# Spectral mixer plus MLP on one core: kept splits of the spectral weights and matrices, and 47-point groups spread over the steps of the unit ahead

## The chip, the cores and the metric

The kernel runs on one core of one Trainium2 chip. The metric is the time of the program on the device in microseconds (us), lower is better. A core has TensorE (PE in the profile, its weight loads as PEld), VectorE (DVE), ScalarE (ACT), GpSimd (POOL) and SyncE (SP), which here only issues transfers. ACT issues transfers too.

## The reference

Inputs are x of 8 x 3008 x 256 and weights in float32. What is computed, cut to what matters:

```python
X = np.fft.rfft(x, axis=1)                      # over the 3008 positions
Yr = Xr @ w_r - Xi @ w_i + b_r
Yi = Xr @ w_i + Xi @ w_r + b_i
Yr, Yi = soft_threshold(Yr, 0.01), soft_threshold(Yi, 0.01)
x = np.fft.irfft(Yr + 1j * Yi, n=3008, axis=1)  # 8 x 3008 x 256
h = np.maximum(x.transpose(0, 2, 1) @ w_tok1, 0) @ w_tok2   # over positions
u = x + h.transpose(0, 2, 1)
out = u + np.maximum(u @ w_ch1, 0) @ w_ch2      # over the 256 features, 1536 wide
```

`soft_threshold` is sign(y) * max(|y| - 0.01, 0).

## The kernel before

The transform of length 3008 = 47 x 64 is done in two stages, and the spectrum never goes back to time order by itself: the token layer's first weight is transformed as well (the "spectral weight", `w_d` in DRAM), and the token layer is applied to the spectrum.

The 8 batch elements form five units: [0], [1], [2,3], [4,5], [6,7], numbered 0 to 4. Each unit has two parts.

- **The 47-point stage** (`dft47`) has 13 groups. Of each group a tile x is loaded, its sum (POOL) and difference (DVE) form the tile sd, sd is split into a high part xh (a cast on ACT) and a low part xl (a subtraction on DVE), `stage1` multiplies it on PE into p, ACT copies p to a and issues the write of a to `a_d` in DRAM. A float32 product is always three matmuls of split operands (`mm3`).
- **The 64-point steps.** There are 12 pairs kp of frequencies, and one step for each pair and batch element. In step n, `forward` makes the transform px, which ACT copies to xf and splits; one step later `mix` multiplies by w_r and w_i (pm), DVE applies bias and threshold (z), ACT and POOL split the result into yh and yl; three or four steps after forward, `inverse` multiplies by the inverse matrix et (pi, written to `b_d`), and after that `tokens` adds the product with the spectral weight wt into the accumulator gp.

wt and et are split pairs. Units 1 to 4 each load the unsplit weight aw from `w_d` and the matrix ef from the input and split them anew for each kp: `split_w` (cast on ACT, subtraction on POOL) and `split_e` (cast on ACT, subtraction on DVE). All splits go through the same helper, so their lines are L146 (cast) and L149 (subtraction). The tiles of sd and of z rotate through the same two buffers (tag "t4"). wt has two buffers, and so has et.

The channel layer works on chunks of up to 512 positions: `make_u` builds u (pu), ph is its first product, hh and hlo its split result, po its second product. Chunks of units 0 to 3 are interleaved with the spectral steps of the units behind them: `spectral(u)` is a generator that yields a cost after each piece of work, and the main loop draws pieces from it while the spectral work that is left (`left_s`) is above its share of the channel work that is left (`left_c`). A yielded "wait" holds it for 10 units of channel work. Unit 0 is done ahead of all, in the part called the begin. From chunk 19 on only channel work is left, in wider chunks. A static scheduler then orders the instructions of each engine.

Loads are issued by SP (`DMA`), writes of a, b, w_d by ACT (`PUT`), each in the order of that engine's program.

Of the kernel before, what the change touches and what calls it, by code (L numbers as in the profile page):

```python
# [24 lines left out]
NG = 13  # L25
# [101 lines left out]
def tile_kernel(ctx: ExitStack, tc: tile.TileContext, io):  # L127
# [16 lines left out]
    def split(hi, lo, src, hi_eng, lo_eng):  # L144
        if hi_eng is S:
            S.copy(out=hi, in_=src)  # L146
        else:
            hi_eng.tensor_copy(out=hi, in_=src)
        lo_eng.tensor_tensor(out=lo, in0=src, in1=hi.bitcast(F32), op=ALU.subtract)  # L149
# [81 lines left out]
    w_d = dram.tile([KP, 128, 2, DT], F32, name="w_d")  # L231
    a_d = [dram.tile([128, KH, 512], F32, name=f"a_d{p}") for p in range(2)]
    b_d = [dram.tile([NSLOT, 96, 512], F32, name=f"b_d{u}") for u in range(len(UNITS))]
    g_d = {u: dram.tile([2, 128, 2 * 2 * C], F32, name=f"g_d{u}") for u in SPILL}


# [6 lines left out]
    def sum_diff(x, g, w, eng, pool):  # L243
        if eng is None:
            return x
        sd = t4([120, 2, w], "sd") if pool is None else wk.tile([120, 2, w], F32, tag=("xtl", "xf", "wt", "et")[g % 4], name="sd", bufs=2)
        eng.tensor_tensor(out=sd[:, 0], in0=x[:, 0], in1=x[:, 1], op=ALU.add)
        V.tensor_tensor(out=sd[:, 1], in0=x[:, 0], in1=x[:, 1], op=ALU.subtract)
        return sd
# [6 lines left out]
    def stage1(sd, dst, g, w, pool):  # L256
        n = GS if g < NG - 1 else N2 - GS * (NG - 1)
        a = ev([120, 2, w], "a") if pool is None else pool.tile([120, 2, w], F32, name="a", bufs=4)
        each = 512 // w
        for i0 in range(0, 2, each):  # L260
            pt = bank("p1")
            for i in range(i0, i0 + each):
                o = (i - i0) * w
                if pool is None:
                    mm3(pt[:, o:o + w], f1r[:, 0, i], f1r[:, 1, i], sd[0][:, i], sd[1][:, i], True, True)
                else:
                    PE.matmul(pt[:120, o:o + w], lhsT=f1[:, i], rhs=sd[:, 0], start=True, stop=False)
                    PE.matmul(pt[:120, o:o + w], lhsT=f1[:, 2 * i], rhs=sd[:, 1], start=False, stop=True)
            S.copy(out=a[:, i0:i0 + each].rearrange("p i w -> p (i w)"), in_=pt[:120])
        rows = dst.rearrange("(i n) k w -> (n k) i w", i=2)  # L270
        PUT.dma_start(out=rows[g * 120:g * 120 + n * KH, :, :w], in_=a[:n * KH])
# [14 lines left out]
    def dft47(load, dst, w, ahead, eng, pool=None, turned=False):  # L286
        xs = [load(g) for g in range(ahead)]
        yield "wait" if eng is G else 0.0
        sds = {}

        def prepare(g):
            if g < NG:
                sds[g] = sum_diff(xs[g], g, w, eng, pool)
                xs[g] = None

        def divide(g):
            if g < NG and pool is None:
                sds[g] = split_x(sds[g], w)

        prepare(0)  # L300
        prepare(1)
        divide(0)
        for g in range(NG):
            if g + ahead < NG:
                xs.append(load(g + ahead))
            prepare(g + 2)
            divide(g + 1)
            if turned:
                stage1_turned(sds.pop(g), dst, g)
            else:  # L310
                stage1(sds.pop(g), dst, g, w, pool)
            yield (SLOW if pool is None else 0.7) * w / C
# [23 lines left out]
    def load_w(src, kp):  # L336
        if src is a_w and kp % 3 == 2:
            aw = wc["early"].tile([128, 2, DT], F32, name="aw")
        else:
            aw = wk.tile([128, 2, DT], F32, tag="lw", name="aw")  # L340
        DMA.dma_start(out=aw, in_=src[:, 2 * kp:2 * kp + 2] if src is a_w else src[kp])
        return aw
# [13 lines left out]
    def load_e(kp):  # L356
        ef = wk.tile([128, 2, 128], F32, tag="le", name="ef")
        DMA.dma_start(out=ef, in_=io["e"][kp].rearrange("p (i j) -> p i j", i=2))
        return ef


    def split_w(wf, eng):
        wt = wk.tile([128, 2, 2, DT], F32R, name="wt")
        split(wt[:, 0], wt[:, 1], wf, S, eng)
        return wt

    def split_e(ef, eng):
        et = wk.tile([128, 2, 2, 128], F32R, name="et")
        split(et[:, 0], et[:, 1], ef, S, eng)
        return et  # L370

    def load_mix():
        wf = wc["wf2"] = const.tile([128, 2, 2, C], F32, tag="gl", name="wf2")
# [47 lines left out]
    def parts(u):  # L421
# [131 lines left out]

        return SimpleNamespace(**{k: v for k, v in locals().items()})

    def spectral(u):
        p = parts(u)
        nb = p.nb
        yield from dft47(p.load_unit, p.a, p.w, 3, V if u == 1 else G)
        yield "wait"  # L560
        steps = [(kp, b) for kp in range(KP) for b in range(nb)]
        a2s, ws, sts, xts, ys = {0: p.load_a(0)}, {}, {}, {}, {}
        for kp in range(2):
            ws[kp] = load_w(w_d, kp), load_e(kp)
        lag = 4 if nb == 1 else 3
        for n in range(len(steps) + lag + nb - 1):
            if n < len(steps):
                kp, b = steps[n]
                if b == 0 and kp + 1 < KP:
                    a2s[kp + 1] = p.load_a(kp + 1)  # L570
                xts[n] = p.forward(kp, b, a2s[kp])
                yield 0.9
            m = n - lag - 1
            if nb == 2 and m >= 0 and m % 2:
                kp = steps[m][0]
                p.tokens(kp, sts.pop(kp)[0], ys.pop(kp))
                yield 2.74
            m = n - 1
            if 0 <= m < len(steps):
                kp, b = steps[m]  # L580
                if b == 0:
                    if nb == 1:
                        t = hl([128, 2, 2, 1, C], "y")
                        ys[kp] = t[:, 0], t[:, 1]
                    else:
                        ys[kp] = hl([128, 2, 2, C], "yh"), hl([128, 2, 2, C], "yl")
                p.mix(kp, xts.pop(m), ys[kp][0][:, :, b], ys[kp][1][:, :, b])
                yield 2.15
            m = n - lag
            if 0 <= m < len(steps) and steps[m][1] == nb - 1:  # L590
                kp = steps[m][0]
                p.inverse(kp, sts[kp][1], ys[kp])
                yield 0.68 * nb
                if nb == 1:
                    p.tokens(kp, sts.pop(kp)[0], ys.pop(kp))
                    yield 1.37
            m = n - 2
            if 0 <= m < len(steps) and steps[m][1] == 0:
                kp = steps[m][0]
                wf, ef = ws.pop(kp)  # L600
                sts[kp] = split_w(wf, G), split_e(ef, V)
                if kp + 2 < KP:
                    ws[kp + 2] = load_w(w_d, kp + 2), load_e(kp + 2)
        p.close()
# [457 lines left out]
    for n, (u, at, cw) in enumerate(chunks):  # L1062
        if n == first_wide:
            channel7(range(n, len(chunks)))
            break
        if at == 0 and u < 2:
            if u == 0:
                left_s = 2.1 * SPECTRAL - spent
                left_c = mixing(0, sum(cu == 0 for cu, _, _ in chunks))
            else:  # L1070
                left_s = sum(len(bs) for bs in UNITS[1:]) * SPECTRAL - spent
                left_c = mixing(n, first_wide - 1)
            pace, hold = 0.0, left_c - (25.0 if u == 0 else 0.0)
        for c in channel(n):
            if c == "end":
                if chunks[n + 1][2] > CW:
                    run(sp)
                    left_s = -1e9
                else:
                    while gts[u + 1] is None:  # L1080
                        step = next(sp)
                        if step != "wait":
                            left_s, spent = left_s - step, spent + step
                continue
            left_c -= c
            if hold is not None:
                if left_c > hold:
                    continue
                pace, hold = left_s / max(left_c, 1.0), None
            while left_s > pace * left_c:  # L1090
                step = next(sp, None)
                if step is None:
                    left_s = -1e9
                elif step == "wait":
                    hold = left_c - 10.0
                    break
                else:
                    left_s, spent = left_s - step, spent + step
# [36 lines left out]
```

## Time and profile before

| | |
|---|---|
| median of 3 runs | 2396.86 us (2394.93 to 2397.55) |
| profiled execution | 2396.32 us, its span 2394.5 us |
| mean granted TensorE clock | 0.999 |
| PE busy | 2366.7 us, 99% of the span |
| PE weight loads busy | 2068.8 us, 86% |
| DVE, ACT, POOL busy | 1384.2, 1128.9, 305.9 us |
| bytes moved by DMA | 253.45 MB |

In rows of the profile, the line L and the names are those of the kernel, "out<-in"; a number in brackets is the time that the engine had been idle before an instruction, with what released it. Durations of successive matmuls overlap, so the time of a stream of matmuls is read from the distance of their starts.

### The profile page before, as it was taken

The page shows a single profiled execution, that of the slowest core. Times are in us where ns is not written, and L with a number is a line of the kernel's source. Part 1 is how long each engine was busy: PE and PEld are TensorE (multiplying, and loading weights), DVE is VectorE, ACT ScalarE, POOL GpSimd, SP SyncE. Part 2 cuts the span into 40 slices and gives each one's busy share as a digit, 9 for nine tenths or more (in the row PEclk, how much of TensorE's full clock was granted, in tenths as well). Part 3 has the DMA queues.
Part 4 walks back from the last instruction along what each step waited for, and adds up shares of the span by engine and source line. Part 5 has one row for each costly group of instructions (what it writes and reads, how often), then busy time and mean ns, then how long its engine had stood idle before and what let it go on. Part 6 is the DMA issues. An engine that isn't in the chain of part 4 may idle for free.

```text
span 2394.5 us, 32230 instructions
## 1 busy us (share of the span) xinstructions
PE 2366.7 (99%) x12578; PEld 2068.8 (86%) x12578; DVE 1384.2 (58%) x2163; ACT 1128.9 (47%) x2016; POOL 305.9 (13%) x259
## 2 busy tenths in 40 slices
PE   8999999999999999999999999999999999999999
PEld 7878999999888889888888888898888889888887
DVE  7976667554454555555555555555555555555554
ACT  6764445444444444354443445444444444444543
POOL 0000332132231232222331000000000000000000
PEclk9999999999999999999999999999999999999999
DMA  8875357433265233563322312022311112221100
GB/s 210 251 220 148 105 166 221 148 108 119 82 191 157 98 111 106 163 199 105 96 82 97 102 55 63 28 81 60 91 57 38 58 52 81 60 88 60 38 1 35
DMA packets 146037, 253.45 MB, mean 106 GB/s; under 512 B 10277, under 2 KB 98429, under 8 KB 145885
## 3 DMA queue, kind: packets, MB, share of 16 engines
q1 hardware_dynamic: 114953, 194.24, 27.2%
q10 hardware_dynamic: 30932, 57.16, 7.5%
q8 instruction: 99, 1.62, 0.3%
q14 instruction: 53, 0.43, 0.1%
HBM read 163.41 MB, written 87.95 MB: 105 GB/s over the span
## 4 chain that ended last, share of the span: by engine, by line
PE 91%; DVE 4%; DMA 2%; ACT 1%; issue 1%; SPq 1%; POOL 0%; ACTq 0%; DVEq 0%; POOLq 0%
PE po L196 10%; PE po L197 10%; PE po L198 10%; PE pu L787 5%; PE ph L196 4%; PE ph L197 4%; PE ph L198 4%; PE px L469 3%; PE sx L196 3%; PE sx L198 3%; PE sx L197 3%; PE pm L196 2%; PE pm L198 2%; PE pm L197 2%; PE pu L196 2%; PE pu L197 2%
## 5 line engine op out<-in xcount | busy, mean ns | idle before, releaser
L196 PE MATMUL po<-hh,w2h 128*128 128x512 f32 (+4 forms) x1176 | 452.4, 385 | 0.0
L197 PE MATMUL po<-hlo,w2h 128*128 128x512 f32 (+4 forms) x1176 | 448.7, 382 | 2.0 <-DVE hlo L826 2.0
L198 PE MATMUL po<-hh,w2l 128*128 128x512 f32 (+4 forms) x1176 | 448.6, 381 | 0.0
L953 ACT ACTIVATE hh<-sn 128x512 fp32r<-128x512 f32 (+2 forms) x360 | 225.6, 627 | 71.1 <-DVE sn L973 46.5
L197 PEld LDWEIGHTS po<-hlo,w2h 128*128 128x128 f32 x1176 | 220.9, 188 | 39.6 <-DVE hlo L826 3.1
L198 PEld LDWEIGHTS po<-hh,w2l 128*128 128x128 f32 x1176 | 220.8, 188 | 38.3
L196 PEld LDWEIGHTS po<-hh,w2h 128*128 128x128 f32 x1176 | 221.0, 188 | 36.8
L954 DVE SCALAR_TENSOR_TENSOR hlo<-sn,hh 128x512 fp32r<-128x512 f32 (+2 forms) x360 | 241.9, 672 | 8.4 <-ACT hh L953 0.7
L825 ACT ACTIVATE hh<-ph 128x512 fp32r<-128x512 f32 (+3 forms) x228 | 129.0, 567 | 220.2 <-PE ph L198 212.8
L826 DVE SCALAR_TENSOR_TENSOR hlo<-ph,hh 128x512 fp32r<-128x512 f32 (+3 forms) x228 | 147.3, 648 | 135.8 <-ACT hh L825 133.8
L962 DVE TENSOR_TENSOR sn<-sq,sn 128x512 f32<-128x512 f32 (+2 forms) x90 | 61.1, 679 | 238.3 <-PE sq L198 218.9
L958 ACT COPY sn<-sx 128x512 f32<-128x512 f32 (+2 forms) x90 | 52.1, 579 | 286.0 <-PE sx L198 285.8
L196 PE MATMUL ph<-uh,w 128*128 128x512 f32 (+3 forms) x456 | 174.4, 383 | 1.7 <-DVE hlo L826 1.5
L197 PE MATMUL ph<-ul,w 128*128 128x512 f32 (+3 forms) x456 | 171.7, 377 | 0.0
L198 PE MATMUL ph<-uh,w 128*128 128x512 f32 (+3 forms) x456 | 171.0, 375 | 0.0
L149 DVE TENSOR_TENSOR xtl<-xf,xth 128x768 fp32r<-128x768 f32 x84 | 83.0, 988 | 112.3 <-ACT xth L146 112.2
L196 PE MATMUL pm<-wmh,xth 128*128 128x256 f32 x504 | 145.5, 289 | 2.4 <-ACT xth L146 2.1
L794 ACT COPY uf<-pu 128x470 f32<-128x470 f32 (+15 forms) x156 | 61.0, 419 | 181.9 <-PE pu L787 181.3
L198 PE MATMUL pm<-wmh,xtl 128*128 128x256 f32 x504 | 142.4, 284 | 0.5 <-DVE xtl L149 0.5
L197 PE MATMUL pm<-wml,xth 128*128 128x256 f32 x504 | 142.2, 283 | 0.0
L787 PEld LDWEIGHTS pu<-g,b 96*128 96x128 f32 x1024 | 130.8, 191 | 3.4
L149 POOL TENSOR_TENSOR yl<-z,yh 128x512 fp32r<-128x512 f32 x72 | 95.4, 1325 | 271.2 <-ACT yh L146 271.2
(185 smaller groups left out, 5106.4 us busy)
## 6 DMA issues: line engine op xcount, KB each, us to landing
wt<-wt_d SPq DMA_DIRECT2D x28, 940.0 KB, 5.7
x<-in_x SPq DMA_DIRECT2D x39, 480.0 KB, 4.9
a<-a_d SPq DMA_DIRECT2D x36, 512.0 KB, 4.6
b_d<-bt ACTq DMA_DIRECT2D x36, 512.0 KB, 4.1
a_d<-a ACTq DMA_DIRECT2D x36, 480.0 KB, 4.3
wt<-wt_d SPq DMA_DIRECT2D x21, 752.0 KB, 5.1
b<-b_d SPq DMA_DIRECT2D x32, 480.0 KB, 6.2
aw<-w_d SPq DMA_DIRECT2D x48, 256.0 KB, 2.7
```

What stands on the lines that cost most here:

```text
L149: lo_eng.tensor_tensor(out=lo, in0=src, in1=hi.bitcast(F32), op=ALU.subtract)
L196: PE.matmul(out, lhsT=wh, rhs=xh, start=start, stop=False, skip_group_check=more)
L197: PE.matmul(out, lhsT=wh, rhs=xl, start=False, stop=False, skip_group_check=more)
L198: PE.matmul(out, lhsT=wl, rhs=xh, start=False, stop=stop, skip_group_check=more)
L469: PE.matmul(pt[:, o:o + 128], lhsT=x, rhs=f2cols(2 * kp + ab), start=True, stop=True)
L787: PE.matmul(pt[:, s * TOKS:(s + 1) * TOKS], lhsT=b2[:, s, cs], rhs=g2[:, 0 if s0 + s == 0 else 1], start=False, stop=s == k - 1)
L794: S.copy(out=ufs[m][:, ct, lo - at:hi - at], in_=pt[:, lo - c0:hi - c0])
L825: S.activation(out=hh, in_=pt, func=AF.Relu)
L826: V.scalar_tensor_tensor(out=hlo, in0=pt, scalar=0.0, in1=hh.bitcast(F32), op0=ALU.max, op1=ALU.subtract)
L953: S.activation(out=hh, in_=t, func=AF.Relu)
L954: V.scalar_tensor_tensor(out=hlo, in0=t, scalar=0.0, in1=hh.bitcast(F32), op0=ALU.max, op1=ALU.subtract)
L962: V.tensor_tensor(out=snap[0], in0=q, in1=snap[0], op=ALU.add)
```

## The change

First, unit 1 writes each pair wt and et that it has split to two new DRAM tensors, `ws_d` (512 KB for each kp) and `es_d` (256 KB), by ACT's queue. Units 2, 3 and 4 load these pairs by SP's queue and split nothing: pairs 0 and 1 at the unit's start, pair kp + 2 right after `tokens(kp)`. Second, units 3 and 4 no longer run the 47-point stage as a stretch of its own ahead of their steps. Its 13 groups are spread over the steps of the unit ahead (2 and 3): at every even step a group is divided and split, at every odd step the next x is loaded and the group's product is made. The split parts xh and xl of these groups lie in other buffers (tag "o") than before; sd stays in "t4". Third, `left_s` is computed from the new sum of costs.

The diff, without the loops that it only repeats:

```diff
+    ws_d = dram.tile([KP, 128, 2 * 2 * DT], F32, name="ws_d")
+    es_d = dram.tile([KP, 128, 2 * 2 * 128], F32, name="es_d")
...
+    def keep_split(kp, wt, et):
+        for kept, t in ((ws_d, wt), (es_d, et)):
+            PUT.dma_start(out=kept[kp], in_=t.rearrange("p a i j -> p (a i j)").bitcast(F32))
+
+    def load_split(kp):
+        wt = wk.tile([128, 2, 2, DT], F32R, name="wt")
+        et = wk.tile([128, 2, 2, 128], F32R, name="et")
+        for kept, t in ((es_d, et), (ws_d, wt)):
+            DMA.dma_start(out=t.rearrange("p a i j -> p (a i j)").bitcast(F32), in_=kept[kp])
+        return wt, et
...
+    def beside(u):
+        p = parts_of(u)
+        xs, sds = {}, {}
+
+        def load(g):
+            if g < NG:
+                xs[g] = p.load_unit(g)
+
+        def divide(g):
+            if g < NG:
+                sd = sum_diff(xs.pop(g), g, p.w, G, None)
+                xh, xl = (wk.tile([120, 2, p.w], F32R, tag="o", name=k, bufs=3) for k in ("xh", "xl"))
+                split(xh, xl, sd, S, V)
+                sds[g] = xh, xl
+
+        def product(g):
+            if g < NG:
+                stage1(sds.pop(g), p.a, g, p.w, None)
...
     def spectral(u):
-        yield from dft47(p.load_unit, p.a, p.w, 3, V if u == 1 else G)
+        if u <= 2:
+            yield from dft47(p.load_unit, p.a, p.w, 3, V if u == 1 else G)
         yield "wait"
...
+        other = beside(u + 1) if u in (2, 3) else None
+        if other:
+            other.load(0)
         for kp in range(2):
-            ws[kp] = load_w(w_d, kp), load_e(kp)
+            if u == 1:
+                ws[kp] = load_w(w_d, kp), load_e(kp)
+            else:
+                sts[kp] = load_split(kp)
         for n in range(len(steps) + lag + nb - 1):
+            if other and n % 2 == 0:
+                other.divide(n // 2)
 ...
+            if other and n % 2:
+                other.load(n // 2 + 1)
...
                 p.tokens(kp, sts.pop(kp)[0], ys.pop(kp))
+                if kp + 2 < KP:
+                    sts[kp + 2] = load_split(kp + 2)
                 yield 2.74
...
+            if other and n % 2:
+                other.product(n // 2)
+                yield 1.4
...
             m = n - 2
-            if 0 <= m < len(steps) and steps[m][1] == 0:
+            if u == 1 and 0 <= m < len(steps):
                 kp = steps[m][0]
                 wf, ef = ws.pop(kp)
                 sts[kp] = split_w(wf, G), split_e(ef, V)
+                keep_split(kp, *sts[kp])
...
-                left_s = sum(len(bs) for bs in UNITS[1:]) * SPECTRAL - spent
+                left_s = 3 * SPECTRAL + 4 * 70.3 - spent
```

The instructions in order. Place one is ACT at the end of the begin, where unit 1's first pairs are split; wf is the transformed weight that goes to `w_d`, wide and raw belong to the MLP weights, a and xh to unit 1's 47-point groups. Before:

```order
L352 ACTIVATE wf<-pw,sc 128x256 x2
L146 CAST wt<-aw 128x512
L353 DMA w_d<-wf 128x512
L146 CAST et<-ef 128x256
L146 CAST wt<-aw 128x512
L352 ACTIVATE wf<-pw,sc 128x256 x2
L146 CAST et<-ef 128x256
L353 DMA w_d<-wf 128x512
L160 ACTIVATE wide<-raw 128x512
L269 COPY a<-p_1290 120x512
L146 CAST xh<-sd 120x512
L271 DMA a_d_91<-a 120x2x256
```

After:

```order
L354 ACTIVATE wf<-pw,sc 128x256 x2
L146 CAST wt<-aw 128x512
L355 DMA w_d<-wf 128x512
L146 CAST et<-ef 128x256
L376 DMA ws_d<-wt 128x1024
L354 ACTIVATE wf<-pw,sc 128x256 x2
L160 ACTIVATE wide<-raw 128x512
L355 DMA w_d<-wf 128x512
L271 COPY a<-p_1292 120x512
L146 CAST xh<-sd 120x512
L273 DMA a_d_91<-a 120x2x256
```

The write of the first kept weight, which waits for POOL's subtraction, stands ahead of the last transformed weight and its write; the casts of the second pair have moved behind this place.

Place two is ACT in one of unit 1's steps: et and wt are the step's pair, b_d takes the inverse's result bt, hh is the channel layer's, xf and xth belong to the next forward, y is the mix's high part. Before:

```order
L146 CAST et<-ef 128x256
L524 DMA b_d_93<-bt 32x8x256
L146 CAST wt<-aw 128x512
L825 ACTIVATE hh<-ph 128x470
L794 COPY uf<-pu 128x470 x2
L471 COPY xf<-px 128x512
L146 CAST xth<-xf 128x768
```

After:

```order
L146 CAST et<-ef 128x256
L537 DMA b_d_93<-bt 32x8x256
L146 CAST wt<-aw 128x512
L376 DMA es_d<-et 128x512
L885 ACTIVATE hh<-ph 128x470
L376 DMA ws_d<-wt 128x1024
L484 COPY xf<-px 128x512
L146 CAST xth<-xf 128x768
```

The write of the matrix stands ahead of hh and the write of the weight behind it, ahead of the copy of px.

Place three is DVE in the steps of unit 2. The four rows of z are one mix's chain; sd and xl are a 47-point group's difference and low part; hlo, uh and ul are the channel layer's; et is the matrix's low part. Before, in a step:

```order
L149 TENSOR_TENSOR et<-ef,et 128x256
L149 TENSOR_TENSOR xtl<-xf,xth 128x768
L826 SCALAR_TENSOR_TENSOR hlo<-ph,hh 128x512
L148 CAST uh<-uf 128x1024
L498 TENSOR_TENSOR z<-pm_6392,bias 128x512
L149 TENSOR_TENSOR ul<-uf,uh 128x1024
L499 TENSOR_TENSOR z<-pm_6393,z 128x512
```

After:

```order
L511 TENSOR_TENSOR z<-pm_6334,bias 128x512
L250 TENSOR_TENSOR sd<-x 120x512
L512 TENSOR_TENSOR z<-pm_6335,z 128x512
L518 TENSOR_SCALAR z<-z 128x512
L149 TENSOR_TENSOR xl<-sd,xh 120x1024
L519 TENSOR_TENSOR z<-z 128x512
L886 SCALAR_TENSOR_TENSOR hlo<-ph,hh 128x512
```

The subtraction of et is gone from the step, and a group's sd and xl now stand within a mix's chain.

In the whole program PE has 11388 instructions both times. DVE has 2129 where it had 2165, POOL 228 for 264, ACT 2115 for 2163 (72 casts fewer, 24 transfers more), SP 456 both times (36 loads of wt and 36 of et for 36 each of aw and ef).

More of the change, by code (lines that the diff above doesn't have):

```diff
@@ L554, in parts, with parts_of @@
         return SimpleNamespace(**{k: v for k, v in locals().items()})
+    ps_of = {}
+    def parts_of(u):
+        if u not in ps_of:
+            ps_of[u] = parts(u)
+        return ps_of[u]
+    def beside(u):
[13 more added lines that the diff above has]
+                stage1(sds.pop(g), p.a, g, p.w, None)
+        return SimpleNamespace(load=load, divide=divide, product=product)
     def spectral(u):
-        p = parts(u)
+        p = parts_of(u)
         nb = p.nb
-        yield from dft47(p.load_unit, p.a, p.w, 3, V if u == 1 else G)
+        if u <= 2:
+            yield from dft47(p.load_unit, p.a, p.w, 3, V if u == 1 else G)
         yield "wait"
```

## The prediction

> **What bounds the kernel now.** I read the page's first lines and its chain, then one table of the four stages, then PE's waits, and last the places that the change touches. In the first line of the fence stands the span, in the second each engine's busy time, in the third the shares of the chain that ended last.
>
> ```profile
> span 2394.5 us, 32230 instructions
> ...
> PE 2366.7 (99%) x12578; PEld 2068.8 (86%) x12578; DVE 1384.2 (58%) x2163; ACT 1128.9 (47%) x2016; POOL 305.9 (13%) x259
> ...
> PE 91%; DVE 4%; DMA 2%; ACT 1%; issue 1%; SPq 1%; POOL 0%; ACTq 0%; DVEq 0%; POOLq 0%
> ```
>
> PE is busy for 99% of the span and has 91% of the chain. Next the stages: the begin (0 to 188), unit 1's spectral steps beside the first channel chunks (188 to 420), units 2 to 4 (420 to 1300), and the channel MLP alone. Columns: stretch, length, busy time and count of PE, PEld, DVE, ACT, POOL, granted clock, DMA share, GB/s.
>
> ```profile
> 0.00:188.00 188.00, 172.41 (x952) 145.52 (x953) 153.64 (x318) 122.05 (x220) 2.74 (x6) 0.99 0.76 222
> 188.00:420.00 232.00, 227.84 (x1384) 210.99 (x1383) 154.25 (x240) 116.49 (x211) 63.01 (x49) 1.00 0.55 163
> 420.00:1300.00 880.00, 876.39 (x4999) 780.36 (x4998) 465.21 (x660) 377.81 (x653) 240.16 (x204) 1.00 0.39 122
> 1300.00:2394.50 1094.50, 1090.06 (x5249) 931.90 (x5247) 611.08 (x947) 512.53 (x934) 0.00 (x0) 1.00 0.20 61
> ```
>
> PE is idle for 15.6, 4.2, 3.6 and 4.4 us in the four. Units 2 to 4, where nearly all of the change lies, have 880.00 - 876.39 = 3.6 us. Its waits there, with the sum, times and longest in us, are three groups; the first of them is a single wait at its very start.
>
> ```profile
> PE po L197 <- DVE hlo L826: 1.8, 1, 1.8
> PE pm L196 <- ACT xth L146: 1.1, 3, 0.4
> PE pm L198 <- DVE xtl L149: 0.5, 1, 0.5
> ...
> 423.99 0.44 PE L197 MATMUL po<-hlo,w2h 128*128 128x376 f32 x1 [1.78 <-DVE hlo L826]
> ```
>
> A busy PE could still be a slow one. So I looked at how far apart matmuls of 512 columns start, in the mixed stage (first pair) and in the last stage (second pair).
>
> ```profile
> 1140.86 0.40 PE L196 MATMUL po<-hh,w2h 128*128 128x512 f32 x1
> 1141.10 0.39 PE L197 MATMUL po<-hlo,w2h 128*128 128x512 f32 x1
> ...
> 1846.03 0.39 PE L198 MATMUL sw<-ub,ws 128*128 128x512 f32 x1
> 1846.26 0.39 PE L196 MATMUL sq<-ub,w 128*128 128x512 f32 x1
> ```
>
> They start 0.24 and 0.23 us apart though each lasts 0.39: the durations overlap and PE streams without a gap. Over all such pairs the mean is 228.2 ns in the mixed stage and 227.0 in the last one. If all matmuls of the mixed stage lose that half per cent, it is 876.39 x 1.2/227.0 = 4.6 us. So what can be won in units 2 to 4 at the very most is 3.6 + 4.6 = 8.2 us, and the PE program itself has as many matmuls after the change as before.
>
> [...]
>
> **The change, part by part. Splits no longer made.** Units 2 to 4 drop 36 times four instructions: two casts on ACT, a subtraction on POOL (the weight) and one on DVE (the matrix). One step of unit 1 shows them, as they stand in every unit:
>
> ```profile
> 279.34 0.41 ACT L146 CAST et<-ef 128x256 fp32r<-128x256 f32 x1
> 279.78 0.84 DVE L149 TENSOR_TENSOR et<-ef,et 128x256 fp32r<-128x256 f32 x1 [0.92 <-ACT et L146]
> 280.16 0.62 ACT L146 CAST wt<-aw 128x512 fp32r<-128x512 f32 x1 [0.41 <-PE gp L198]
> 280.91 1.30 POOL L149 TENSOR_TENSOR wt<-aw,wt 128x512 fp32r<-128x512 f32 x1 [0.57 <-POOL y L149]
> 281.32 0.56 ACT L825 ACTIVATE hh<-ph 128x470 fp32r<-128x470 f32 x1 [0.54 <-PE ph L198]
> 283.49 0.59 ACT L471 COPY xf<-px 128x512 f32<-128x512 f32 x1 [1.61 <-PE px L469]
> ```
>
> That is 36 x 1.03 = 37 us of ACT, 36 x 1.30 = 47 us of POOL and 36 x 0.84 = 30 us of DVE, out of 377.81, 240.16 and 465.21. All of it lies beside PE's 876.39. What it can give back is PE's waits on ACT and DVE in that stage: 1.1 + 0.5 = 1.6 us (the 1.8 at 424 is before the first unit with kept splits is under way). I take **-1.5**; the ends are 0 and -8.2 (every idle moment and the slower streaming gone).
>
> **Loads in their place.** A step's load grows from 256 + 128 KB to 512 + 256 KB, so 36 x 384 KB = 13.8 MB more, and unit 1 writes 12 x 768 KB = 9.4 MB. Rows of the view of DMA issues (engine, count, KB each, median us to landing):
>
> ```profile
> a<-a_d SPq DMA_DIRECT2D x36, 512.0 KB, 4.6
> b_d<-bt ACTq DMA_DIRECT2D x36, 512.0 KB, 4.1
> ...
> aw<-w_d SPq DMA_DIRECT2D x48, 256.0 KB, 2.7
> ef<-in_e SPq DMA_DIRECT2D x60, 128.0 KB, 4.0
> ...
> w_d<-wf ACTq DMA_DIRECT2D x12, 256.0 KB, 3.8
> ```
>
> By the code a pair is asked for right after tokens(kp), when the buffers come free, and first read by inverse(kp+2), three steps later. The stage runs 3 x 24 steps in 880 us, 12 us each, so the cover is 36 us against the 4.6 of a 512 KB load. SP stands at the issue until tokens has ended; behind it are the next a, x and out transfers, needed a step or more later. The DMA share is 0.39 there. **0**; if the cover were gone it would be a landing at each of three unit starts.
>
> **47-point groups moved.** 26 groups of units 3 and 4 keep every instruction: sum on POOL, difference and low part on DVE, cast, copy and a_d issue on ACT, six matmuls on PE, one x load on SP. The first two are, in this stage (count, busy us, mean ns, idle before):
>
> ```profile
> L247 POOL TENSOR_TENSOR sd<-x 120x512 f32<-120x512 f32 x26 | 42.8, 1645 | 73.9 <-DVE xl L149 72.4 <-DMA ef<-in_e 1.2
> ...
> L149 DVE TENSOR_TENSOR xl<-sd,xh 120x1024 fp32r<-120x1024 f32 x28 | 36.2, 1292 | 25.3 <-ACT xh L146 23.3 <-DMA g_d<-gl 1.6
> ```
>
> A group's split is asked for a step ahead of its product, 12 us, and needs about 1.65 + 1.29 us and a cast: hidden. A late x load would hold POOL and DVE, but x is fetched a step ahead too. What changes is a shared buffer. The group's sd and the output z of the 64-point mixing rotate through the same two buffers, so around each sd two successive z share one, and the second's first DVE instruction has to wait until POOL has read the first. In before one such chain is:
>
> ```profile
> 880.33 0.69 DVE L498 TENSOR_TENSOR z<-pm,bias 128x512 f32<-128x512 f32 x1 [2.48 <-PE pm L198]
> ...
> 883.69 0.62 ACT L146 CAST yh<-z 128x512 fp32r<-128x512 f32 x1
> 884.38 1.28 POOL L149 TENSOR_TENSOR yl<-z,yh 128x512 fp32r<-128x512 f32 x1 [2.77 <-ACT yh L146]
> ```
>
> From 880.33 to 885.66 it takes 5.3 us. Two mixings are usually a 12 us step apart; by the order of PE, two stand close, with a p group of six matmuls (6 x 0.23 = 1.4 us) and a px between, only at two places. There DVE could stand 5.3 - 1.4 = 3.9 us at the most, and behind it the hlo that PE waits for, part of it covered by work already queued. Ends 0 and +2.6 (a stall such as the 1.78 of hlo at one place, half of it at the other); I take **+0.5**, nearer to 0 since those waits were 1.8 in all in this stage before.
>
> **The begin.** The first kept weight (512 KB) is issued on ACT right after the first two casts, ahead of the last w_d write. The rows there, in before:
>
> ```profile
> 141.27 0.62 ACT L146 CAST wt<-aw 128x512 fp32r<-128x512 f32 x1 [2.20 <-DMA aw<-w_d]
> 141.97 1.27 POOL L149 TENSOR_TENSOR wt<-aw,wt 128x512 fp32r<-128x512 f32 x1 [141.53 <-ACT wt L146]
> ...
> 144.49 0.33 ACTq L353 DMA_DIRECT2D w_d<-wf  x1
> 145.09 0.32 SPq L341 DMA_DIRECT2D aw<-w_d  x1
> 145.71 0.33 SPq L358 DMA_DIRECT2D ef<-in_e  x1
> ...
> 150.74 0.59 ACT L269 COPY a<-p 120x512 f32<-120x512 f32 x1 [3.29 <-DMA w_d<-wf]
> 151.66 0.48 PE L196 MATMUL pu<-wt,gh 128*128 128x470 f32 x1 [2.51 <-ACT gh L547]
> ```
>
> The w_d write issued at 144.49 landed just before 150.74, 6.2 us later against a median of 3.8: the queues are crowded. ACT's copy waited 3.29 us for it, and through gh PE waited 2.51. Now 512 KB go ahead of it from 143.24 (141.97 + 1.27), and the aw and ef loads (384 KB) that ran beside it come later. Ends: +4.1, the whole landing of a 512 KB write put ahead, and -2.5, the stall gone. The middle is +0.8; I take **+1.0**, since the write goes first and is the larger.
>
> **Unit 1 keeps its splits.** ACT issues two more transfers per step, 24 in all. An issue takes it 0.33 us (the row of w_d above). The one of the matrix waits for DVE's subtraction, that of the weight for POOL's, which ends at 280.91 + 1.30 = 282.21, in the step above. ACT's next work that needs the steps, the copy of px, came at 283.49 after 1.61 us of idle time; so the issue at 282.2 fits into it, and the hh behind it is needed by PE a group later. Where the issue stood ahead of hh, ACT would stand 1.3 us, at most 12 x 1.30 = 15.6 us. I take **+0.5**, nearest to the step's own row (1.61 idle), ends 0 and +7.8 (half of 15.6 reaching PE).
>
> [...]
>
> **Sum:** -1.5 + 0 + 0.5 + 0.5 + 1.0 = +0.5 us. The profiled execution took 2396.32, 1.8 around its span, and 0.5 less than the median of the runs, 2396.86. On it the sum gives 2396.8, and against the median **2397.4**: no change that can be measured (0.2%, 4.8 us, is about what a measurement of this kernel can tell).
>
> **Rivals.** (1) Slower: ACT stands at each ws_d issue for POOL. The place is the twelve steps of unit 1, the price half of 15.6 in place of 0.5, so 2397.4 + 7.3 = 2404.7. It decides once ACT's idle time there, 1.61 in the row above, falls below the 1.30 and the hh queued behind. (2) The begin: the w_d write lands a full 4.1 later, 2397.4 + 3.1 = 2400.5, still no change. (3) Faster: all of the begin's 2.5, the 1.6 of waits and half of the slower streaming (2.3) go, and nothing comes: 2396.86 - 6.4 = 2390.5. For it speaks that ACT and POOL lose about a tenth and a fifth of that stage's work; against it, that PE hardly waits for them. [...] (5) The change doesn't spread the load but delays it: kept splits land late at each of three unit starts, 3 x 4.6 = 13.8, so 2410.7; the 36 us of cover speak against it.
>
> **How the numbers follow.** Forecast 0.57, (2) 0.12: same 0.69. (3) 0.10 and (4) 0.03: faster 0.13. (1) 0.12 and (5) 0.06: slower 0.18. The terms' own ends, without (1), reach from 2396.86 - 8.2 - 2.5 = 2386.2 to 2396.86 + 4.1 + 2.6 = 2403.6. The range 2387.5 to 2405 holds the forecast, (1), (2) and (3), and leaves out (4), (5) and the tails of (1) and (3), some 0.15.
>
> **What would show it.** PE's busy time unchanged at about 876 for the same matmuls; ACT and POOL in units 2 to 4 down by 37 and 47 us; PE's idle time in that stage between 2 and 4 us; the wait of pu for gh at about 151 us between 0 and 6.6; rows of z that wait for POOL with no row of PE behind them; and in unit 1 ws_d issues in ACT's idle time. I am wrong if PE's waits in unit 1's steps pass 4 us, if hlo or an et from es_d heads PE's waits after 420, or if 512-column matmuls start clearly less than 228 ns apart on the mean.

## The result and the profile after

The changed kernel takes 2405.1 us (median of 6 runs, 2404.25 to 2406.27), the kernel before 2396.85 (2394.93 to 2398.72): a ratio of 1.0034, 95% interval 1.0024 to 1.0044. It is slower by 8.25 us. The forecast of no measurable change was wrong, and 2405.1 lies 0.1 above the top of its range. The profiled execution took 2406.16 us, against 2396.32 before. First the page of the profile after: span, busy times, chain.

```profile
span 2404.4 us, 32093 instructions
...
PE 2368.9 (99%) x12578; PEld 2069.7 (86%) x12578; DVE 1362.6 (57%) x2127; ACT 1097.8 (46%) x1944; POOL 249.4 (10%) x223
...
PE 90%; DMA 4%; DVE 4%; ACT 1%; SPq 1%; issue 0%; POOL 0%; ACTq 0%; DVEq 0%; POOLq 0%
```

PE has the same work; DVE, ACT and POOL have less; the chain's share of DMA has doubled from 2% to 4%. To find the place, both executions are cut at the same points of the program: at the last po matmul of chunks 0, 2, 3 and 18. The first table is before, the second after (columns as in the prediction's table).

```profile
0.00:194.00 194.00, 178.41 (x986) 150.98 (x987) 158.21 (x327) 125.18 (x226) 2.74 (x6) 0.99 0.76 221
194.00:316.30 122.30, 118.80 (x748) 109.38 (x747) 75.17 (x121) 56.80 (x101) 30.00 (x26) 1.00 0.40 122
316.30:372.90 56.60, 56.34 (x349) 52.33 (x348) 38.49 (x57) 27.08 (x52) 19.09 (x15) 1.00 0.61 177
372.90:1345.40 972.50, 968.50 (x5485) 863.26 (x5484) 526.76 (x752) 424.51 (x736) 254.09 (x213) 1.00 0.42 130
```

```profile
0.00:196.10 196.10, 177.82 (x986) 149.82 (x987) 159.02 (x327) 123.90 (x225) 2.78 (x6) 1.00 0.78 227
196.10:318.40 122.30, 118.92 (x747) 109.29 (x746) 75.15 (x121) 57.01 (x100) 28.81 (x25) 1.00 0.49 153
318.40:381.00 62.60, 59.31 (x350) 54.73 (x350) 36.09 (x55) 26.24 (x49) 18.81 (x14) 0.95 0.72 227
381.00:1355.30 974.30, 968.22 (x5485) 862.91 (x5484) 506.56 (x718) 395.04 (x667) 199.04 (x179) 1.00 0.47 144
```

The lengths differ by +2.1, 0, **+6.0** and +1.8 us; the rest, 1049.1 us, is equal. So the largest part lies in one chunk of 57 us, in unit 1's steps, and there the granted clock is 0.95. PE's waits in that chunk, and two windows of it behind the wait:

```profile
PE pm L196 <- DVE hlo L886: 3.3, 1, 3.3
...
333.00:339.40 6.40, 6.11 (x22) 5.61 (x23) 5.51 (x12) 2.80 (x5) 1.64 (x1) 0.52 0.96 270
339.40:345.00 5.60, 5.60 (x37) 5.23 (x36) 2.18 (x4) 2.60 (x5) 2.88 (x3) 1.00 0.94 274
```

One stall of 3.3 us (0.3 at that place before), and behind it PE runs at a granted clock of 0.52 for 6.4 us and at 1.00 after that: about 3.0 us of stall and 2.9 of slow clock make the 6.0 of this execution. Waits after that chunk, in units 2 to 4 (420 to 1300):

```profile
PE po L197 <- DVE hlo L886: 2.3, 2, 1.8
PE pm L196 <- ACT xth L146: 1.1, 3, 0.4
PE po L196 <- DVE o L946: 0.9, 1, 0.9
```

They are 4.3 us where they were 3.4: nothing was won there although POOL's busy time fell by 55.1 us (254.09 to 199.04), ACT's by 29.5 and DVE's by 20.2.

### The profile page after: what moved, and what is told of

Its sections match the earlier page's. It is cut to its first block, busy times and chain, and to the rows that moved or that the text cites. A ratio compares the mean times of both kernels' runs of the same rounds, so it can differ in the third digit from the quotient of the medians.

```text
span 2404.4 us, 32093 instructions
## 1 busy us (share of the span) xinstructions
PE 2368.9 (99%) x12578; PEld 2069.7 (86%) x12578; DVE 1362.6 (57%) x2127; ACT 1097.8 (46%) x1944; POOL 249.4 (10%) x223
## 3 DMA queue, kind: packets, MB, share of 16 engines
q8 instruction: 99, 1.62, 0.3%
## 4 chain that ended last, share of the span: by engine, by line
PE 90%; DMA 4%; DVE 4%; ACT 1%; SPq 1%; issue 0%; POOL 0%; ACTq 0%; DVEq 0%; POOLq 0%
PE po L197 10%; PE po L196 10%; PE po L198 10%; PE pu L847 4%; PE ph L196 4%; PE ph L197 4%; PE ph L198 4%; PE px L482 3%; PE sx L196 3%; PE sx L197 3%; PE sx L198 3%; PE pm L196 2%; PE pm L198 2%; PE pm L197 2%; PE pu L196 2%; PE pu L197 2%
```

## The experiments

The runs of the kernel before that stand beside them gave medians of 2396.11 us (for the first four), 2396.24 (the next four) and 2396.57 (the last four).

**The two halves apart, and the issue that I suspected.** In the stretch before the stall ACT stood at the write of pair 8's weight (issued at 331.12, 1.9 us after the cast) with hh right behind it (331.49, after 2.25 us of idle time that POOL's wt ended). My first theory was that this standing makes the stall. Four runs: each half of the change alone, that issue moved to SP, and that issue added to the kernel before.

Kept splits alone (`kept_only`):

```diff
-        if u <= 2:
-            yield from dft47(p.load_unit, p.a, p.w, 3, V if u == 1 else G)
+        yield from dft47(p.load_unit, p.a, p.w, 3, V if u == 1 else G)
-        other = beside(u + 1) if u in (2, 3) else None
+        other = None
-                left_s = 3 * SPECTRAL + 4 * 70.3 - spent
+                left_s = sum(len(bs) for bs in UNITS[1:]) * SPECTRAL - spent
```

> The first half of the change alone: unit 1 keeps its splits and units 2 to 4 load them, the 47-point stages of units 3 and 4 stay a stretch ahead of their steps, as before. Theory A (the loss is made by the twelve kept-weight issues of unit 1, which ACT holds for POOL: mostly the one at about 331 us, 3.0 us of PE stall and 2.9 us at half clock behind it, and some 2 us in the begin): +6 to +8 on 2396.85, so 2403 to 2405, and a PE wait for hlo of about 3.4 us near 330 us. Theory B (the loss is made by the spread groups): -1 to +2, so 2396 to 2399.

Measured: 2402.47 us, ratio 1.0024 (1.0013 to 1.0035), a PE wait of 3.2 us for hlo at the same place.

Spread groups alone (`spread_only`):

```diff
-            if u == 1:
-                ws[kp] = load_w(w_d, kp), load_e(kp)
-            else:
-                sts[kp] = load_split(kp)
+            ws[kp] = load_w(w_d, kp), load_e(kp)
...
-            if u == 1 and 0 <= m < len(steps):
+            if 0 <= m < len(steps) and steps[m][1] == 0:
...
-                keep_split(kp, *sts[kp])
```

> The second half alone: the 47-point groups of units 3 and 4 are spread, every unit loads and splits its weights and matrices as before, nothing is kept. Theory A: no stall near 330 us; what is left are the waits that the changed order makes after 420 us (about 1.0 at 472 and 1.5 at 1329 in the changed kernel, against about 1.5 fewer elsewhere), so 0 to +2.5 on 2396.85, 2397 to 2399.5. Theory B: +5 to +8, 2402 to 2405.

Measured: 2398.21, ratio 1.0010 (1.0000 to 1.0019), a wait of 0.5 us at that place. So the first half carries +6.4 us and the second +2.1 (0 to 4.6 by its interval); together that is 8.5, against 8.25 for the change.

The issue of pair 8 moved (`one_moved`) and, in the kernel before, added (`before_one`):

```diff
-            PUT.dma_start(out=kept[kp], ...)
+            (DMA if kp == 8 and t is wt else PUT).dma_start(out=kept[kp], ...)
```

> The changed kernel with one issue moved: the kept weight of pair 8 is written by SP's queue in place of ACT's; the order of PE's matmuls is the same. Theory A: ACT goes straight to hh, the PE stall of 3.45 us and the half clock behind it go, 2405.1 - 5.9 = 2399.2 (2398.3 to 2400). Theory A without the clock (the slow stretch after the stall has another cause, such as the DMA traffic there): 2405.1 - 3 = 2402. Theory B: 2404 to 2406.

```diff
                 sts[kp] = split_w(wf, G), split_e(ef, V)
+                if u == 1 and kp == 8:
+                    PUT.dma_start(out=ws_d, in_=sts[kp][0].rearrange("p a i j -> p (a i j)").bitcast(F32))
```

> The kernel before with one added issue: in unit 1, the split weight of pair 8 is also written to DRAM by ACT's queue, which puts the issue ahead of hh as in the changed kernel; nothing reads it; the order of PE's matmuls is that of before. Theory A: +5.9, 2402.7, with a PE wait for hlo of about 3.4 us near 331 us and a granted clock of 0.5 for some 6 us behind it. Theory A without the clock: +3, 2399.9. Theory B: no change, 2396.9.

Measured: 2405.92, 1.0035 (1.0023 to 1.0047), and 2398.47, 1.0008 (0.9998 to 1.0017). My theory on this issue fell: with the write on SP, the stall (3.0 us) and the half clock (0.50 to 0.57 over 6.4 us) stayed. DVE and ACT of `one_moved` at that place:

```profile
327.94 0.56 ACT L885 ACTIVATE hh<-ph 128x470 fp32r<-128x470 f32 x1
...
329.64 1.61 DVE L169 TENSOR_TENSOR wide<-raw,wide 128x376 f32<-128x376 f32 x1
...
332.36 0.64 DVE L886 SCALAR_TENSOR_TENSOR hlo<-ph,hh 128x470 fp32r<-128x470 f32 x1
```

The hlo that PE waits for comes late although its hh, at 327.94, had long been done: DVE was late itself, working off a row of instructions on wide, the unpacked MLP weight. That led further up. The rows of before, from 306 us:

```profile
306.35 0.33 SPq L179 DMA_DIRECT2D raw<-in_wt  x1
309.69 0.55 ACT L162 ACTIVATE raw<-raw 128x376 f32<-128x376 uint32 x1 [0.49 <-DMA raw<-in_wt]
311.29 0.69 DVE L506 TENSOR_TENSOR z<-z 128x512 f32<-128x512 f32 x1
311.90 0.64 DVE L826 SCALAR_TENSOR_TENSOR hlo<-ph,hh 128x470 fp32r<-128x470 f32 x1
316.31 0.38 SPq L179 DMA_DIRECT2D raw<-in_wt  x1
319.47 0.55 ACT L160 ACTIVATE wide<-raw 128x376 f32<-128x376 f32 x1 [1.29 <-DMA raw<-in_wt]
```

And after, 2.2 us later in time by what the begin lost:

```profile
307.89 0.33 ACTq L376 DMA_DIRECT2D ws_d<-wt  x1
308.51 0.33 SPq L179 DMA_DIRECT2D raw<-in_wt  x1
313.31 0.56 ACT L162 ACTIVATE raw<-raw 128x376 f32<-128x376 uint32 x1 [1.91 <-DMA raw<-in_wt]
313.76 0.55 ACT L885 ACTIVATE hh<-ph 128x470 fp32r<-128x470 f32 x1
314.35 0.65 DVE L886 SCALAR_TENSOR_TENSOR hlo<-ph,hh 128x470 fp32r<-128x470 f32 x1 [1.62 <-ACT hh L885]
314.91 0.68 DVE L519 TENSOR_TENSOR z<-z 128x512 f32<-128x512 f32 x1
315.63 0.62 ACT L146 CAST y<-z 128x512 fp32r<-128x512 f32 x1 [1.31 <-DVE z L519]
316.63 0.41 ACT L146 CAST et<-ef 128x256 fp32r<-128x256 f32 x1
319.47 0.36 ACTq L376 DMA_DIRECT2D ws_d<-wt  x1
319.89 0.37 SPq L179 DMA_DIRECT2D raw<-in_wt  x1
324.91 0.55 ACT L160 ACTIVATE wide<-raw 128x376 f32<-128x376 f32 x1 [2.71 <-DMA raw<-in_wt]
326.37 0.65 DVE L886 SCALAR_TENSOR_TENSOR hlo<-ph,hh 128x470 fp32r<-128x470 f32 x1 [1.97 <-ACT hh L885]
...
332.60 0.64 DVE L886 SCALAR_TENSOR_TENSOR hlo<-ph,hh 128x470 fp32r<-128x470 f32 x1
```

Two loads of raw (376 KB) are waited for by ACT. Before, they land 3.3 and 3.2 us after their issue (309.69 - 306.35, 319.47 - 316.31). After, each starts 0.4 to 0.6 us behind a 512 KB write of a kept weight, and they take 4.8 and 5.0. And DVE's order has changed: z stood ahead of hlo, now hlo, which waits for hh, which waits for raw, stands ahead of z. So the first delay goes on through y, et and wt to SP's queue (the next ef and aw loads wait for the splits of et and wt: ef is issued at 317.92, where DVE's et ends at 317.89, and aw at 319.46, where POOL's wt ends at 319.44; the second raw is issued right behind aw, at 319.89): the two are 11.4 us apart where they were 10.0. Both delays add up to 1.4 + 1.9 = 3.3 us. Behind the second raw DVE waits 1.97 us for hh (326.37), in before 0.16; its instructions on wide come later by that, and after them the hlo that PE waits for (332.60). This was theory C, against theory D, that ACT's standing at pair 7's issue (319.47, 1.2 us behind the end of the issue before it) makes the difference.

**Pairs 6 and 7.** Pair 7's weight written by POOL's queue in place of ACT's:

```diff
-            PUT.dma_start(out=kept[kp], ...)
+            (G if kp == 7 and t is wt else PUT).dma_start(out=kept[kp], ...)
```

> The changed kernel with one issue moved: the kept weight of pair 7 (at 319.5 us) is written by POOL's queue, so that ACT doesn't stand there; the same bytes go at about the same moment, and PE's order is the same. Theory C (traffic: a 512 KB write that starts just ahead of a load of raw makes it land late, first by 1.4 us for pair 6, then by 1.9 for pair 7; ACT waits for raw with hh queued behind it, and PE stalls 3.3 us at 333 us): the stall stays between 2.5 and 3.4 us, 2402 to 2405. Theory D (ACT's own 1.2 us of standing at pair 7 makes the difference): the stall falls to 2.1 us or less and the half clock behind it goes, about 2400.

Measured: 2404.48, 1.0034 (1.0021 to 1.0046), a stall of 2.2 us with some 3 us at about half clock behind it; the second raw took 4.5 us to land in place of 5.0. The time says C; the stall lies between the two. ACT's standing may have a part of it; the rest stays with the issue moved.

Pairs 6 and 7 not kept:

```diff
-                keep_split(kp, *sts[kp])
+                if kp not in (6, 7):
+                    keep_split(kp, *sts[kp])
...
+                if kp + 2 in (6, 7):
+                    wf, ef = load_w(w_d, kp + 2), load_e(kp + 2)
+                    sts[kp + 2] = split_w(wf, G), split_e(ef, V)
```

> The changed kernel without keeping pairs 6 and 7: unit 1 doesn't write them, units 2 to 4 load and split them as before the change; PE's order is the same. Theories C and D: raw lands after some 3 us at both places, the stall at 333 us shrinks to 0.7 us or less, 2405.1 - 3 to - 6, so 2399 to 2402. If the loss comes from elsewhere (the other ten writes, the loads of the kept pairs, the spread groups): 2404 to 2406.

Measured: 2402.08, 1.0024 (1.0014 to 1.0034), just above the range of C and D, a stall of 0.4 us. The two pairs have their part; more than half of the loss is still there in the median, so it is not all.

The weights of both pairs, and of pair 7 alone, written in the kernel before (`kp in (6, 7)` or `kp == 7` in the edit of before_one):

> The kernel before with two added issues: in unit 1 the split weights of pairs 6 and 7 are also written to DRAM by ACT's queue, at the places where the changed kernel writes them; nothing reads them; PE's order is that of before. Theory C: raw lands 1.4 and 1.9 us later, a PE stall of about 3.3 us at 331 us, +3 to +6 with the clock: 2399 to 2402. Theory D: about half of it, +1.2, 2397.5. If the loss comes from elsewhere: 2396.

> The same with pair 7 alone. Theory C: only the second raw is late, by 1.9 us, and a PE stall of 1.5 to 2.2 us at 329 us follows, too short for the clock to fall: +1.5, 2397.5 to 2398.5. Theory D: the same as with both pairs.

Measured: 2397.17, 1.0004 (0.9994 to 1.0013), and 2396.85, 1.0005 (0.9996 to 1.0014). Neither is told from the kernel before; the stalls are 1.3 us in both. C was half wrong here. The raws of before_two took 4.6 and 4.8 us to land, nearly as long as in the change, but they were issued 9.9 us apart, and by its order DVE has z ahead of hlo, so that the first delay ended there:

```profile
311.48 0.69 DVE L507 TENSOR_TENSOR z<-z 128x512 f32<-128x512 f32 x1
312.14 0.65 DVE L829 SCALAR_TENSOR_TENSOR hlo<-ph,hh 128x470 fp32r<-128x470 f32 x1
```

So lateness alone doesn't suffice here; the order has to hand it on.

**The same with both writes of a pair, all pairs, the writes elsewhere, and fewer bytes.** With the matrices' writes too, the scheduler puts hlo ahead of z in the kernel before as well. `b67`:

```diff
                 sts[kp] = split_w(wf, G), split_e(ef, V)
+                if u == 1 and kp in (6, 7):
+                    for kept, t in ((ws_d, sts[kp][0]), (es_d, sts[kp][1])):
+                        PUT.dma_start(out=kept[kp], in_=t.rearrange("p a i j -> p (a i j)").bitcast(F32))
```

> The kernel before with both writes (matrix and weight) of pairs 6 and 7 added in unit 1; nothing reads them; PE's order is that of before. With them the order of DVE has hlo ahead of the last z of pair 6's mix, as in the changed kernel, where before and with the weights' writes alone it has z first. Theory C2 (the writes make raw land 1.4 to 1.9 us later, and hlo, which waits for it through hh, now stands ahead of z, so the first delay passes through y, bt, et and ef to the issue of the second raw; both add up): raw loads 11.4 us apart in place of 10.0, PE stall of 3.2 to 3.5 us near 331 us, half clock behind it in some executions, +3 to +6: 2399 to 2402.5. If the order doesn't matter: a stall of 1.4 us as with the weights alone, +1, 2397.

Measured: 2400.47, 1.0016 (1.0006 to 1.0026). The raws, DVE's order and PE's wait:

```profile
304.43 0.33 SPq L179 DMA_DIRECT2D raw<-in_wt  x1
315.52 0.37 SPq L179 DMA_DIRECT2D raw<-in_wt  x1
308.94 0.55 ACT L162 ACTIVATE raw<-raw 128x376 f32<-128x376 uint32 x1 [1.66 <-DMA raw<-in_wt]
320.81 0.54 ACT L160 ACTIVATE wide<-raw 128x376 f32<-128x376 f32 x1 [2.98 <-DMA raw<-in_wt]
...
309.97 0.65 DVE L831 SCALAR_TENSOR_TENSOR hlo<-ph,hh 128x470 fp32r<-128x470 f32 x1 [1.35 <-ACT hh L830]
310.53 0.68 DVE L508 TENSOR_TENSOR z<-z 128x512 f32<-128x512 f32 x1
...
PE pm L196 <- DVE hlo L831: 3.3, 1, 3.3
```

The whole chain, in a kernel that is otherwise the one before: 4.5 and 5.3 us to land, 11.1 us apart, a stall of 3.3, and +3.9 us.

All twelve pairs written, nothing read (`ball`, the same edit with `kp >= 0`):

> The kernel before with all twelve pairs written in unit 1 as in the change, and nothing else of it: nothing reads them, every unit splits its own, the 47-point stages stay. If the writes make the loss of the first half of the change (kept splits alone: 2402.5), this is 2401 to 2404; if the loads of the kept pairs share in it, 2399 or less.

Measured: 2402.92, 1.0032 (1.0021 to 1.0043), the same stall of 3.3 us. The writes alone, with no kept pair ever loaded, give +6.35 us, as much as the first half of the change.

The writes moved to unit 2 (`keep_in_2`):

```diff
-            if u == 1 and 0 <= m < len(steps):
+            if u <= 2 and 0 <= m < len(steps) and steps[m][1] == 0:
...
-                keep_split(kp, *sts[kp])
+                if u == 2:
+                    keep_split(kp, *sts[kp])
```

> The changed kernel with the writes moved: units 1 and 2 split for themselves, unit 2 writes the pairs, units 3 and 4 load them; spread groups as in the change. Theory C2: nothing is written in the begin and in unit 1, so raw lands in time there, no stall over 0.7 us near 331 us; what is left is the spread groups' part, 2397 to 2399. If the loss lies in loading kept pairs or wherever they are written: 2402 or more.

Measured: 2397.32, 1.0007 (0.9998 to 1.0015), a stall of 0.5 us at that place. With the same bytes written at another time, and the kept pairs loaded in two units in place of three, the change can't be told from the kernel before.

Small writes (`small_67`, not_67 with the two pairs' writes put back at 64 columns each; `small` is set for these two):

```diff
+            if small:
+                PUT.dma_start(out=kept[kp][:, :64], in_=flat[:, :64])
```

> The changed kernel in which unit 1 issues the writes of pairs 6 and 7 at the same places, each with 64 columns (32 KB) in place of 512 and 256 KB, and units 2 to 4 split these two pairs for themselves. Theory C2 (bytes on the way): raw lands 3.2 to 3.4 us after its issue at both places, in place of 4.8 and 5.0, although ACT stands at the issue of pair 7's weight as long as before; stall near 331 us 1.5 us or less. If the standing or the issues themselves do it: raw lands in time but the stall stays above 2 us.

Measured: 2400.03, 1.0015 (1.0006 to 1.0023), a stall of 0.3 us. The raws:

```profile
307.84 0.33 SPq L179 DMA_DIRECT2D raw<-in_wt  x1
317.77 0.37 SPq L179 DMA_DIRECT2D raw<-in_wt  x1
311.70 0.55 ACT L162 ACTIVATE raw<-raw 128x376 f32<-128x376 uint32 x1 [0.99 <-DMA raw<-in_wt]
321.04 0.55 ACT L160 ACTIVATE wide<-raw 128x376 f32<-128x376 f32 x1 [1.36 <-DMA raw<-in_wt]
```

They land after 3.9 and 3.3 us with the issues in place and the bytes gone. The first is a little late still; the second is as in before. But DVE's order is not the changed kernel's: in small_67, as in not_67 and keep_in_2, the traces have z ahead of hlo again. These three runs take away the late raws and the order together. Late raws without that order are before_two; the order with raw in time was not run. That it would cost little alone is argued: in the changed kernel hlo waits 1.62 us at that place, about what raw is late by.

## Why the prediction was wrong

- **What bounds the kernel**: right. PE's matmuls, their busy time and their pace are unchanged. Over the 512-column pairs of units 2 to 4 (420 to 1300 us) that follow without a pause, the mean start distance is 228.2 ns after and 228.2 before, so the faster side, given 0.13, is out: ACT, POOL and DVE lost work and PE's pace stayed.
- **Splits no longer made, -1.5**: wrong in sign, by little. The work left the engines (POOL -55 against 47 forecast), but the 1.1 us of waits for xth stayed, the 0.5 for xtl went, and 1.4 of others came.
- **The shared buffer, +0.5**: seen as described. At 467.81 DVE's z had stood 2.07 us for POOL's yl, and the o behind it cost PE 0.9 at 471.66. The second half's +2.1 us (0 to 4.6 by its interval) is more than this explains; the rest of it was not placed.
- **The begin, +1.0**: not borne out, and not settled. Its end moved from 194.0 to 196.1. The wait of pu for gh at about 151 us fell from 2.5 to 1.2, but waits of PE of 1.5 us for a group's xl (0.3 before) and 1.0 for an xh came. The ends of single executions differ for another reason too: before has 3.4 us at half clock in this part (0.52 from 41.0 to 44.4), after none. With half of such stretches taken off (an estimate) it ends at 192.3 in before and at 191.9, 192.9 and 193.7 in b67, spread_only and keep_in_2, where this part is as before the change; of those that write here as the change does, ball ends at 190.8, one_moved at 192.9, and the changed kernel at 196.1. By these the writes of the begin cost nothing that shows in more than one trace.
- **Unit 1 keeps its splits, +0.5**: this is the step that failed. It asked only whether ACT has time for the issue, and took one step's 1.61 us of idle time for all twelve. The writes in fact cost 6.35 us (ball), which lies within the term's ends, 0 and +7.8, but not for their reason. I had looked for a price in POOL's subtraction; it lay in the 512 KB themselves: a load that ACT waits for, issued 0.4 to 0.6 us behind them, landed 1.4 to 1.9 us late.
- **Loads in their place, 0**: right for the loads (keep_in_2 and PE's waits show none for a kept pair). But the 9.4 MB of writes were set against a DMA share of 0.39, that of units 2 to 4. They fall into unit 1's steps, whose row in my own table says 0.55, and where two loads of raw were already waited for in the trace of before, 0.49 and 1.29 us.
- **Rival (1)** had the side, the place (unit 1's steps) and almost the time, 2404.7, by the wrong mechanism: with the issue of pair 8 off ACT the time stayed at 2405.9, and with pair 7's at 2404.5. That the range, drawn to hold this rival, ends within 0.1 us of the result is luck.
- **The signs of being wrong**: two came. PE's waits in unit 1's steps (188 to 420 us) are 7.1 us, past the 4 that I had set, though before had 4.2 already; and hlo heads PE's waits after 420, with 2.3 us, as it did before with 1.8. The first pointed at the right place.

Where the 8.25 us are: about 3.9 by the writes of pairs 6 and 7 (b67; taking their bytes out of the changed kernel won 2.4 in not_67 and 4.8 in small_67), some 2.5 by the other ten (ball less b67, with intervals that overlap), and about 2 by the spread groups or what goes with them. The 2.5 have no place in the trace: cut at the same points, ball's profiled execution (2399.3, the fastest of its seven) has stretches of 192.5, 121.7, 60.1, 973.8 and 1049.2 us against 194.0, 122.3, 56.6, 972.5 and 1049.1 before, and only the one with the stall is longer by more than 1.5.

## What to carry to other kernels

Here a write that nothing waits for had a price where it ran beside a load that is waited for: behind 512 KB the two raws took 4.8 and 5.0 us to land in place of 3.3 and 3.2. So look in the trace of before for loads that end an engine's idle time near the place of a new write, and price their lateness, not the issue. A lateness that stays inside one engine's slack can be free, as in before_two (raws of 4.6 and 4.8 us, ratio 1.0004); ask which instruction in the next queue stands behind the late one, since with hlo, which waited, ahead of z, which was ready, the delays added up to a stall of 3.3 us in the changed kernel. And keep the writing of kept data for a stretch that loads nothing urgent: written in unit 2, and so loaded in two units only, it measured +0.75 us in place of +8.25.

## What the hardware showed beyond that

The same stall did not always cost the same. Behind it the granted clock fell to about half for 6 us in the changed kernel (0.52) and in one_moved (0.50 to 0.57), for about 3 in b67 and pair7_on_pool, and not at all in ball and kept_only (1.00), with stalls of 3.3, 3.0, 3.3, 2.2, 3.3 and 3.2 us. The rows of pair7_on_pool, b67 and ball from the stall's end:

```profile
329.20:331.00 1.80, 1.80 (x8) 1.80 (x9) 1.80 (x5) 0.65 (x2) 0.00 (x0) 0.50 0.85 241
...
329.00:332.00 3.00, 2.83 (x13) 2.83 (x14) 3.00 (x7) 1.69 (x4) 0.73 (x1) 0.57 0.95 257
332.00:335.00 3.00, 3.00 (x14) 2.61 (x14) 2.97 (x6) 0.89 (x2) 0.00 (x0) 0.86 1.04 244
...
329.00:332.00 3.00, 2.81 (x17) 2.50 (x18) 3.00 (x8) 1.40 (x3) 0.70 (x1) 1.00 0.92 246
```

By these six, the length of the stall alone does not decide. A shorter one can do it: the wait of 1.8 us for hlo that the prediction shows at 424 us stands in all fourteen traces, and in nine of them some 3 us of half clock begin within 2 us of its end, in five (before, after, one_moved, before_two and spread_only) none. In b67:

```profile
426.81 0.44 PE L197 MATMUL po<-hlo,w2h 128*128 128x376 f32 x1 [1.78 <-DVE hlo L831]
...
428.50:431.70 3.20, 3.20 (x11) 2.71 (x10) 2.35 (x4) 1.17 (x2) 0.00 (x0) 0.50 0.10 34
```

So the 1.5 to 2.2 us that I had called too short for the clock to fall are not, by the 1.8 us here and the 2.2 of pair7_on_pool. Nor do they always suffice: in before the granted clock is 1.00 behind the 1.78 us at 424 (424 to 436) and behind PE's wait of 2.51 us at 151.66 (151.7 to 158). What decides between the two these traces do not show.
